# Reordering kv and num on TensorE and moving a copy of v to ScalarE in a linear-attention and MLP kernel

## The chip, the cores and the metric

The kernel runs on one core of a Trainium2 chip. The metric is the device time of one execution in microseconds (us); a version's time is the median of its runs. All runs here are fast, at a granted clock of 0.997 to 1.0. A ratio of two kernels is the mean time of one kernel's fast runs over that of the other's of the same rounds, so it is not quite the ratio of the medians that are quoted beside it. A position in a profile is in us from the start of its span.

Engine names: PE is TensorE (matmul), PEld its weight loads, DVE VectorE, ACT ScalarE, POOL GpSimd, SP the queue that issues most stores and copies. L366 is line 366 of the kernel's file; after the change lines below 190 lie up to 5 further down (L199 is then L202, L366 is L371, L387 is L392), and in e5 4 more. An instruction is "due" at the time at which it would start if nothing but the matmuls ahead of it on TensorE held it up.

## The reference, cut to what matters

```python
# q, k, v: (8 batches, 8 heads, 576 positions, 64)
q_p, k_p = phi(q), phi(k)                      # phi(x) = where(x > 0, x, exp(x) - 1) + 1
kv  = einsum('bhsd,bhse->bhde', k_p, v)
z   = sum(k_p, axis=2)
num = einsum('bhsd,bhde->bhse', q_p, kv)
den = einsum('bhsd,bhd->bhs', q_p, z)[..., None] + 1e-06
x   = (num / den) transposed to (4608, 512)
h   = x @ w_in                                 # layer 1, 2048 wide
out = (h - tanh(h)) @ w_out                    # layer 2
```

## The kernel before

The 4608 rows go through the two layers in 9 chunks of 512. A chunk has a layer 1 of 16 tiles of four matmuls and a layer 2 of 16 steps of four matmuls. The attention of the next batches is hung between them: `s1[i]` holds what is issued behind tile `i` of layer 1, `s2[i]` what is issued behind step `i` of layer 2. The program order is the order on each engine.

```python
def a_qT_pe(b, i, banks, on=None):          # transposes of phi(q), 2 x (matmuls, then a copy by ACT or DVE)
    ...
def a_kv(b, banks):                         # 36 matmuls (64 rows) of kp and v, then kz = kv * mask on DVE
    ...
def a_vp(b, i):                             # v repacked for the later batches
    nc.vector.tensor_copy(vp[:, i, :, 0:128]..., v_b[b % 2][:, 0:2, i])

def a_kv_cols(b, banks):                    # kv from vp, later batches
    ps = [banks()[:, 0:272]... for hg in range(2)]
    for i in range(2):
        for j in range(J):
            for hg in range(2):
                nc.tensor.matmul(ps[hg][:, i, :], kp[...], vp[...], ...)
    for hg in range(2):
        nc.vector.tensor_mul(kz_t[b][:, hg, :, 0:136], ps[hg], mask[...])

def a_den(b, banks):                        # 16 small matmuls with kz, then + 1e-6 and reciprocal on DVE
    ...
def a_spread(b):                            # the reciprocal goes to memory (ds) and comes back on 128 partitions (rdb)
    for t in range(4):
        nc.sync.dma_start(out=ds[:, t, :], in_=rden_t[b][32 * t:32 * t + H, :])
    for hh in range(2):
        nc.sync.dma_start(out=rdb[64 * hh:64 * hh + 64]..., in_=ds[...]...partition_broadcast(64))

def a_num(b, p):                            # num from kz into one of two PSUM banks; DVE scales it by rdb into xT
    ...

# chunk 0 (batch 1)
s2[7].append(lambda: (a_qT_pe(1, 0, side), a_qT_pe(1, 1, side), a_kv(1, side)))
s2[8].append(lambda: b0_scale_rest(side))
s2[9].append(lambda: a_den(1, side))
s2[10].append(lambda: (num1(), a_split(1)))   # split: four DVE steps from the reciprocal to w
s2[11].append(lambda: spread1(0))             # batch 1 is spread by matmuls of w, not through memory
s2[12].append(lambda: q2(0))                  # phi of q of batch 2
...
# chunk 1 (batch 2)
s1[1].append(lambda: a_kphi(2, 1))
s1[3]: a_vp(2, 0), a_vp(2, 1)
s1[7].append(lambda: a_kv_cols(n1, attn))
s1[10].append(lambda: (a_den(n1, attn), a_spread(n1)))
s2[11 + p].append(lambda p=p: a_num(n1, p))   # p = 0 .. 4

# layer 1, behind the four matmuls of tile fi
elif fi % 2:
    n = dense.order[(dense.n - 1) % 6]        # six PSUM banks, three pairs of tiles
    l1act2(fi - 1, ps_all[:, n - 1:n + 1, :], gT)   # tanh on ACT, subtraction on DVE
for f in s1[fi]:
    f()
```

## Time and profile before

| | before |
|---|---|
| median, range of the first 3 runs | 295.44, 295.11 to 295.50 us |
| PE, DVE, ACT busy | 97%, 60%, 48% of the span |
| matmul of 512 columns, start to start | 0.216 us |
| gaps in the PE stream where the change works | 0.72, 0.86 and 0.53 us |

The three gaps are shown and worked out in the prediction below. One more piece of the same kernel's timeline turns out to matter (start, duration, engine, line, operation; in brackets the idle time ahead and what ended it):

```profile
65.45 1.29 SPq L305 DMA_DIRECT2D ds<-rden  x4
70.65 1.12 SPq L308 DMA_DIRECT2D rdb<-ds  x2
...
79.10 1.89 DVE L328 TENSOR_TENSOR xT<-ps_all,rdb 128x512 bf16<-128x512 f32 x3 [2.26 <-DMA rdb<-ds]
...
79.85 0.38 PE L317 MATMUL ps_all<-qT,kz 128*128 128x512 bf16 x1
```

The reciprocal of batch 2 leaves for memory at 65.45, comes back by 79.1, and only then can VectorE scale the first num. The third num needs the PSUM bank of the first. It was due at 79.81 (78.95, the start of the matmuls ahead of it, + 4 x 0.216) and starts at 79.85: before the change, this broadcast is only just on time.

### The profile page before, as it was taken

What the parts mean: (1) busy time and instruction counts of PE and PEld (TensorE: products, weight loads), DVE (VectorE), ACT (ScalarE), POOL (GpSimd) and SP (SyncE); (2) the same over time, 40 slices, a digit from 0 to 9 for tenths busy, and PEclk for the clock granted to TensorE, in tenths of its full rate; (3) what the DMA queues carried; (4) which work ended last, traced back from release to release, by engine and by line L of the source; (5) the groups of instructions that cost most, each with busy time, mean ns of one, the idle gap of its engine ahead of it and who ended that gap; (6) DMA issues with size and microseconds to landing.
All of it is one profiled execution on the core that took longest, in us unless ns stands there. A gap on an engine that the chain in (4) does not pass through costs nothing.

```text
span 293.2 us, 4504 instructions
## 1 busy us (share of the span) xinstructions
PE 285.2 (97%) x1801; PEld 134.3 (46%) x1801; DVE 174.6 (60%) x265; ACT 139.6 (48%) x168; POOL 33.3 (11%) x55
## 2 busy tenths in 40 slices
PE   8899999999999999999999999999999999999994
PEld 2544453454444444444444445444444444444443
DVE  4759857887567764786478646865581456106600
ACT  4938536947344643455246524661552155126411
POOL 8673030030030003000300020000000000000000
PEclk9999999999999999999999999999999999999999
DMA  6999999998999758955895669667117310131032
GB/s 101 194 204 212 208 207 216 200 145 153 234 163 185 160 118 139 218 117 129 136 223 127 139 134 183 134 154 143 38 24 178 73 36 0 38 84 24 0 74 72
DMA packets 39077, 38.94 MB, mean 133 GB/s; under 512 B 16336, under 2 KB 33808, under 8 KB 38288
## 3 DMA queue, kind: packets, MB, share of 16 engines
q0 software_dynamic: 17552, 18.35, 38.6%
q1 hardware_dynamic: 21344, 20.17, 30.3%
q8 instruction: 14, 0.23, 0.3%
q10 hardware_dynamic: 160, 0.13, 0.1%
q14 instruction: 7, 0.06, 0.1%
HBM read 43.91 MB, written 9.55 MB: 182 GB/s over the span
## 4 chain that ended last, share of the span: by engine, by line
PE 79%; DMA 11%; issue 7%; POOL 2%; DVE 0%; ACT 0%; POOLq 0%
PE ps_all L387 37%; PE ps_all L366 36%; DMA qraw<-in_q_dram 6%; DMA w_in_sb<-in_moe_w_in_dram 3%; PE ps_all L199 2%; DMA kraw<-in_k_dram 2%; PE ps_all L317 2%; PE ps_all L604 1%; PE ps_all L276 1%; POOL qraw L90 0%; ACT e L134 0%; POOL kraw L93 0%; DVE qp L136 0%; POOL v L93 0%; POOL w_out_sb L115 0%
## 5 line engine op out<-in xcount | busy, mean ns | idle before, releaser
L366 PE MATMUL ps_all<-xT,w_in_sb 128*128 128x512 bf16 x576 | 128.0, 379 | 0.3 <-DVE xT L244 0.3
L387 PE MATMUL ps_all<-w_out_sb,gT 128*128 128x512 bf16 x560 | 127.8, 379 | 0.0
L373 DVE TENSOR_TENSOR gT<-ps_all,th 128x1024 bf16<-128x1024 f32 x64 | 77.9, 1218 | 59.8 <-ACT th L372 59.8
L372 ACT ACTIVATE th<-ps_all 128x1024 f32<-128x1024 f32 x64 | 65.5, 1024 | 57.0 <-PE ps_all L366 47.1
L366 PEld LDWEIGHTS <-w_in_sb 128*128 128x128 bf16 x576 | 55.3, 98 | 66.6 <-issue 0.6
L387 PEld LDWEIGHTS <-gT 128*128 128x128 bf16 x560 | 54.1, 98 | 64.3 <-issue 0.3
L396 ACT COPY osb<-ps_all 128x512 f32<-128x512 f32 (+1 forms) x36 | 20.9, 583 | 73.4 <-PE ps_all L387 54.2
L328 DVE TENSOR_TENSOR xT<-ps_all,rdb 128x512 bf16<-128x512 f32 x24 | 16.3, 689 | 13.4 <-PE ps_all L317 11.2
L134 ACT ACTIVATE e<-qraw 128x1152 bf16<-128x1152 bf16 x16 | 18.5, 1162 | 6.9 <-DMA qraw<-in_q_dram 6.9
L134 ACT ACTIVATE e<-kraw 128x1152 bf16<-128x1152 bf16 x15 | 17.5, 1166 | 0.2 <-DMA kraw<-in_k_dram 0.2
L136 DVE TENSOR_TENSOR qp<-e,r 128x1152 bf16<-128x1152 bf16 x16 | 12.0, 757 | 7.8 <-ACT e L134 7.2
L136 DVE TENSOR_TENSOR kp<-e,r 128x1152 bf16<-128x1152 bf16 x15 | 11.4, 759 | 8.3 <-ACT e L134 7.5
L383 POOL COPY g<-qT 1x1 bf16<-1x1 bf16 x5 | 1.2, 240 | 120.6 <-DMA qT<-qp 120.6
L378 DVE TENSOR_TENSOR gT<-ps_all,th 128x512 bf16<-128x512 f32 x16 | 10.3, 685 | 2.4 <-ACT th L377 1.7
L377 ACT ACTIVATE th<-ps_all 128x512 f32<-128x512 f32 x16 | 9.2, 598 | 4.3 <-PE ps_all L366 3.1
L317 PE MATMUL ps_all<-qT,kz 128*128 128x512 bf16 x28 | 10.1, 379 | 0.0
L444 PE MATMUL ps_all<-zero 128*128 128x512 bf16 x29 | 8.8, 463 | 1.2 <-DVE zero L405 1.2
L135 DVE TENSOR_SCALAR r<-qraw 128x1152 bf16<-128x1152 bf16 x16 | 7.3, 453 | 2.2 <-DMA qraw<-in_q_dram 2.2
L199 PE MATMUL ps_all<-vp,kp 64*128 64x136 bf16 x216 | 7.4, 220 | 0.4 <-POOL g L383 0.4
L199 PEld LDWEIGHTS <-kp 64*128 64x128 bf16 x216 | 6.4, 94 | 3.0 <-issue 2.1
L285 DVE RECIPROCAL rden<-den 128x144 f32<-128x144 f32 x7 | 7.4, 1053 | 0.2
L394 DVE COPY osb<-ps_all 128x128 f32<-128x128 f32 x1 | 0.3, 292 | 11.6 <-PE ps_all L604 11.6
(82 smaller groups left out, 121.7 us busy)
## 6 DMA issues: line engine op xcount, KB each, us to landing
out_dram<-osb SPq DMA_DIRECT2D x70, 128.0 KB
rdb<-ds SPq DMA_DIRECT2D x12, 576.0 KB
kraw<-in_k_dram POOLq DMA_DIRECT2D x7, 576.0 KB, 7.1
qraw<-in_q_dram POOLq DMA_DIRECT2D x7, 576.0 KB, 9.0
v<-in_v_dram POOLq DMA_DIRECT2D x7, 576.0 KB, 12.2
w_out_sb<-in_moe_w_out_dram POOLq DMA_DIRECT2D x4, 512.0 KB, 16.4
w_in_sb<-in_moe_w_in_dram POOLq DMA_DIRECT2D x6, 256.0 KB, 8.6
qraw<-in_q_dram POOLq DMA_DIRECT2D x2, 288.0 KB, 4.6
```

The lines of the kernel that those rows point to most:

```text
L134: return (lambda: nc.scalar.activation(e, x, AF.Exp), lambda: nc.vector.tensor_scalar(r, x, 0.0, 1.0, ALU.max, ALU.add), lambda: nc.vector ...
L136: lambda: nc.vector.tensor_tensor(y, e, r, ALU.min))
L199: nc.tensor.matmul(ps[hg][:, i, :], kp[r, i, j].rearrange("p h d -> p (h d)"), vp[r, i, j, :], start=(j == 0), stop=(j == J - 1))
L317: nc.tensor.matmul(ps, kz[:, p // 2, p % 2, 0:128], qT[:, p % 2, 0:8, p // 2, :], start=True, stop=True)
L328: nc.vector.tensor_mul(xT[:, p, S * b:S * b + 512].rearrange("p (j t c) -> p j t c", j=8, t=4), ps.rearrange("p j (t c) -> p j t c", t=4), ...
L366: nc.tensor.matmul(h, w_in_sb[:, 2 * (p % 2) + p // 2, fi * 128:(fi + 1) * 128], xT[:, p, c * 512:(c + 1) * 512], start=(n == 0), stop=(n ...
L372: nc.scalar.activation(th, h, AF.Tanh)
L373: nc.vector.tensor_sub(gT[:, fi:fi + 2, :], h, th)
L377: nc.scalar.activation(th, h, AF.Tanh)
L378: nc.vector.tensor_sub(gT[:, fi, :], h, th)
L387: nc.tensor.matmul(o, gT[:, fi, i * 128:(i + 1) * 128], w_out_sb[:, fi, :], start=(fi == 0), stop=(fi == NF - 1))
L396: nc.scalar.copy(osb[:, f0:f1], o[:, f0:f1])
```

## The change

Its intent: fill the wait for phi(q) in chunk 0 with kv, which needs no q; let num run beside den, so that the wait for the num copies closes; in chunk 1, take the copies of v off VectorE, and put kv later and in two halves, so that it does not wait for them.

```diff
+    def a_vp_act(b, i):
+        nc.scalar.copy(vp[:, i, :, 0:128].rearrange("p j (h d) -> p h j d", h=2), v_b[b % 2][:, 0:2, i])
-    def a_kv_cols(b, banks):
+    def a_kv_cols(b, banks, i_s=(0, 1), ps=None):
-        ps = [banks()[:, 0:272].rearrange("p (i e) -> p i e", i=2) for hg in range(2)]
-        for i in range(2):
+        ps = ps or [banks()[:, 0:272].rearrange("p (i e) -> p i e", i=2) for hg in range(2)]
+        for i in i_s:
 (cut: the matmuls)
+        if i_s == (0,):
+            return ps
 (cut: kz)
-            s2[7].append(lambda: (a_qT_pe(1, 0, side), a_qT_pe(1, 1, side), a_kv(1, side)))
+            s2[7].append(lambda: (a_qT_pe(1, 0, side), a_kv(1, side), a_qT_pe(1, 1, side)))
-            s2[9].append(lambda: a_den(1, side))
-            s2[10].append(lambda: (num1(), a_split(1)))
+            s2[9].append(lambda: (a_den(1, side), num1(), a_split(1)))
-            s2[12].append(lambda: q2(0))
-            s2[13].append(lambda: (spread1(1), q2(1)))
-            s2[14].append(lambda: q2(2))
-            s2[15].append(lambda: a_kphi(2, 0))
+            s2[13].append(lambda: (spread1(1), q2(0)))
+            s2[14].append(lambda: q2(1))
+            s2[15].append(lambda: (q2(2), a_kphi(2, 0)))
-            s1[7 if c == 1 else 5].append(lambda: a_kv_cols(n1, attn))
-            s1[10 if c == 1 else 8].append(lambda: (a_den(n1, attn), a_spread(n1)))
+            if c == 1:
+                s1[8].append(lambda: sub.update(kv=a_kv_cols(n1, attn, (0,))))
+                s1[9].append(lambda: a_kv_cols(n1, attn, (1,), sub["kv"]))
+            else:
+                s1[5].append(lambda: a_kv_cols(n1, attn))
+            s1[11 if c == 1 else 8].append(lambda: (a_den(n1, attn), a_spread(n1)))
-            s1[1].append(lambda: a_kphi(2, 1))
-            for i in range(2):
-                s1[3].append(lambda i=i: a_vp(2, i))
+            k21 = phi_pieces(2, k_t, kp_t, "kp", 1)
+            s1[1].append(k21[0])
+            s1[3].append(lambda: (k21[1](), k21[2](), a_vp_act(2, 0)))
+            s1[5].append(lambda: a_vp_act(2, 1))
```

## The prediction

> **What bounds the kernel now.** I read the page first: engine busy times, then the chain that ended last, then TensorE's waits, then the timeline of the two stretches that the change touches, and last the DMA issues with their times to landing.
>
> ```profile
> PE 285.2 (97%) x1801; PEld 134.3 (46%) x1801; DVE 174.6 (60%) x265; ACT 139.6 (48%) x168; POOL 33.3 (11%) x55
> ```
>
> TensorE is busy 97% of 293.2 us, with modelled ends. The chain of waits, from 59 us on, holds almost nothing but matmuls, 64 of a layer in 13.81 us, so 0.216 us each back to back. No matmul is removed by the change. It can only close gaps in TensorE's stream, and can only open others. TensorE's waits name the gaps:
>
> ```profile
> PE ps_all L164 <- DVE qp L136: 0.8, 2, 0.6
> PE ps_all L354 <- ACT ns L344: 0.7, 1, 0.7
> PE ps_all L199 <- POOL g L383: 0.4, 1, 0.4
> ```
>
> All three are in the stretch that the change rearranges. The timeline (start, duration, instruction) shows them in place:
>
> ```profile
> 37.94 0.68 PE L164 MATMUL ps_all<-ident,qp 128*128 128x128 bf16 x9
> 39.17 0.68 PE L164 MATMUL ps_all<-ident,qp 128*128 128x128 bf16 x9 [0.56 <-DVE qp L136]
> 39.78 1.66 PE L177 MATMUL ps_all<-v,kp 64*128 64x192 bf16 x36
> 41.37 1.04 PE L387 MATMUL ps_all<-w_out_sb,gT 128*128 128x512 bf16 x4
> ...
> 46.17 0.37 DVE L298 SCALAR_TENSOR_TENSOR w<-t,part,u 128x144 bf16<-128x144 bf16 x1
> 47.26 0.31 PE L354 MATMUL ps_all<-w,sel 32*128 32x144 bf16 x8 [0.69 <-ACT ns L344]
> ...
> 51.30 7.07 PE L366 MATMUL ps_all<-xT,w_in_sb 128*128 128x512 bf16 x32
> ...
> 58.23 0.82 DVE L189 COPY vp<-v 128x1152 bf16<-128x1152 bf16 x2
> 58.74 1.24 PE L199 MATMUL ps_all<-vp,kp 64*128 64x136 bf16 x36 [0.37 <-POOL g L383]
> ```
>
> Gap one: the first nine transposes take 9 x 0.057, to 38.45; the next come at 39.17: 0.72. Gap two: the matmuls before the spread (L354) end at 46.40, it starts at 47.26: 0.86; the reciprocal's split is done at 46.54, the last num copy at 47.20. Gap three: layer 1 runs 32 x 0.216 from 51.30, to 58.21, and kv starts at 58.74: 0.53. The label says GpSimd, but its gate feeds only loads; what kv reads is vp, whose first half VectorE ends at 58.64. Together 2.1 us, 0.7% of the time: the most that can be won.
>
> **What the Trainium skill says.** "Trace Analysis", section Per-instruction lifecycle, says that the profiled window of a GpSimd-issued DMA ends when descriptors are generated, not when data has moved. So arrival must be read from the times to landing. These two loads are issued at 22.28 and 23.01:
>
> ```profile
> v<-in_v_dram POOLq DMA_DIRECT2D x1, 576.0 KB, 16.5
> w_out_sb<-in_moe_w_out_dram POOLq DMA_DIRECT2D x1, 512.0 KB, 18.3
> ```
>
> v of batch 1 lands at 38.8, and the third quarter of w_out, which the layer-2 matmuls after kv read, at 41.3. "ScalarE: Activation LUTs", section What ACT_TABLE_LOAD costs, gives 186 ns + 0.833 ns per element, with 93 ns overlap of neighbours: 1146 ns for 1152 elements. The trace agrees: its exp of 1152 takes 1.16 to 1.20, start to start 1.06. Nothing shows this copy on ScalarE before, so I take the exp's figure for it. The same page's Rules for kernel authors has VectorE up to about 3x faster for bf16; here the vp copy on VectorE is 0.45, a factor of 2.6. "TensorEngine Tiling (Array Packing)", section Key Properties, says that changing the tiling mode drains TensorE. The trace fits: in an undisturbed chunk kv takes 1.17 to the next dense matmul, where 36 x 0.0287 (136 columns, two row tiles at once, at 0.42 ns per column, as 512 columns in 0.216) is 1.03; so leaving it costs about 0.15.
>
> ```profile
> 87.46 1.17 PE ps_all L199 x36
> 88.63 2.70 PE ps_all L366 x12
> 91.33 0.36 PE ps_all L276 x16
> ```
>
> **The change, part by part.** The instruction order per engine confirms the same matmuls, reordered; VectorE loses two vp copies, ScalarE gains two.
>
> *Chunk 0, kv between the transposes.* kv needs v, and that lands at 38.8, so it starts at about 38.85, not 38.46. With its 1.59 (39.78 to 41.37 now) it ends at 40.44; the second transposes take 0.51, to about 41.0. But the next layer-2 matmuls need w_out, landing at 41.3. They start at about 41.36, as now at 41.37. So gap one only moves: 0.3 before kv, 0.3 before those matmuls. Gain: 0.
>
> *num beside den.* den stays at 43.3, so its VectorE work to w still ends at 46.54. num comes 0.86 earlier (four matmuls), at 43.7, and its copies end at 46.3, no longer last. The two layer-2 groups now follow num and end at 43.3 + 0.36 + 0.1 + 0.97 + 1.73, about 46.5. The spread starts behind w at 46.68, not 47.26. Gain: 0.58. Layer 1 of chunk 1 starts at 50.72. Moving the query work of batch 2 one step later brings ScalarE into this order: eviction, exp, eviction, exp, eviction, exp of k; at its spacings now (0.47, 1.06) the last eviction starts at 51.93 and the exp at 52.40.
>
> *Chunk 1, vp on ScalarE.* The first tanh runs at 53.46, the second exp of k at 54.36, the second tanh at 55.42 to 56.44, the first copy at 56.32, tanh, the second copy at 58.28, ended by 59.45. The kernel gives layer 1 six PSUM banks, three pairs of tiles: the seventh tile needs the first subtraction, ended at 54.54 + 1.22 = 55.76; it is due at 50.72 + 24 x 0.216 = 55.90, so it just passes. The ninth needs the second subtraction, ended at 57.72; due at 57.63: wait of about 0.15. Gap three (0.53) is gone, since kv comes behind the ninth tile at 58.64.
>
> *kv in two halves.* A second tiling change, 0.15. First half 58.64 to 59.30, tile ten to 60.17, second half to 60.83, tiles eleven and twelve to 62.56, den due at 62.67. Here I see a new wait. den needs kz, the masked product on VectorE. In the new order it stands behind the subtraction of tiles nine and ten. That one follows their tanh (60.37 to 61.39) and the earlier subtraction (60.42 to 61.55): it runs from 61.55, kz from 62.68 to 63.46. den's last twelve matmuls wait for this and end at 63.78 instead of 63.03: 0.75. Now kz starts at 61.23 and den (62.60) does not wait.
>
> Sum: -0.58 - 0.53 + 0.15 + 0.15 + 0.75 = -0.06, with about 0.1 to 0.2 of error in the terms. Layer 2 of chunk 1 starts at about 67.4, as now at 67.46. From there all is the same. With the time before at 295.44, I predict 295.2, leaning a little to the gain because two of my losses (0.15 and 0.75) rest on a chain of starts and the gain rests on one.
>
> **The rivals.** *All gaps close* (the intent): -2.0, 293.4. Against it stand the two landings and w's own end. *The landings don't bind*, if kv may start at 38.46 and w_out is in time: den comes about 0.7 earlier, the spread near 46.0, 294.5. For it: landing times may vary by tenths, and now nothing waits there. Against: the load queue is full throughout (its share is 1.23 of 16 engines between 20 and 40 us), and the change touches no earlier load. *kz is not late*, if VectorE catches up: 294.5. Against: the order puts tanh, subtraction, kz one behind the other, 3.3 us after tile ten, and den only 2.5 us after it. *ScalarE becomes the bound of the start of chunk 1*: the seventh tile has 0.14 of slack; a copy slower than 1.15, or a late eviction, makes each following tile wait: 296 or a little over. For it: ScalarE has 2.1 us more work within the first ten tiles.
>
> **Range and chances.** The rivals lie between 293.4 and 296; the likeliest two misses (each 0.7 to 0.9) go opposite ways. So 294.2 to 296.0 in 8 of 10. A change of 2% would be 5.9 us, almost three times all gaps there are: faster 0.01, within 2% 0.98, slower 0.01.
>
> **What the profile after should show.** The wait at L164 for qp gone; kv in chunk 0 waiting for the load of v until 38.8; the first layer-2 matmuls behind the transposes still at 41.3 to 41.4; the spread 0.5 to 0.7 earlier and released by w, not by the num copies; no wait for vp; two ScalarE copies of about 1.15 each; den of chunk 1 waiting about 0.7 for kz; layer 2 of chunk 1 within 0.4 of 67.46. I am wrong if that stage starts before 66.9 (a landing or kz was no limit) or after 68 (ScalarE holds up PSUM).

## The result, and the profile after

| | before | after |
|---|---|---|
| median of 4 runs of the same rounds | 295.27 us | 295.60 us |
| range | 294.72 to 295.50 | 295.51 to 295.71 |
| ratio after to before | | 1.0014 (95%: 0.9997 to 1.0031) |
| the same kernel again in later rounds (e11) | | 1.0027 (1.0015 to 1.0040) |

The time is inside the predicted range and class, but a few tenths of a us above the kernel before, where I had leaned to a few tenths below. In the first rounds that loss is not clear of noise (the interval holds 1); in those of e11 it is. The waits of TensorE in the changed kernel (us in total, times, longest) no longer have the three of before:

```profile
PE ps_all L322 <- DVE xT L333: 0.5, 1, 0.5
...
PE ps_all L281 <- DVE kz L207: 0.3, 1, 0.3
PE ps_all L392 <- DMA w_out_sb<-in_moe_w_out_dram: 0.2, 1, 0.2
```

In their place stand a wait of den (L281) for kz, one of layer 2 for the load of w_out, and one of num (L322) for the scaling of an earlier num. The timeline of the changed kernel, with the same places as in the prediction and those of the new waits:

```profile
38.29 0.67 PE L164 MATMUL ps_all<-ident,qp 128*128 128x128 bf16 x9
...
39.02 1.43 PEld L177 LDWEIGHTS <-kp 64*128 64x128 bf16 x36 [0.25 <-DMA v<-in_v_dram]
...
40.62 0.68 PE L164 MATMUL ps_all<-ident,qp 128*128 128x128 bf16 x9
...
41.53 1.02 PE L392 MATMUL ps_all<-w_out_sb,gT 128*128 128x512 bf16 x3 [0.24 <-DMA w_out_sb<-in_moe_w_out_dram]
...
46.75 0.12 PEld L359 LDWEIGHTS <-sel 32*128 32x128 bf16 x8 [0.53 <-DVE w L303]
...
58.35 1.19 ACT L192 COPY vp<-v 128x1152 bf16<-128x1152 bf16 x1
...
58.80 0.71 PE L202 MATMUL ps_all<-vp,kp 64*128 64x136 bf16 x18
...
62.77 0.78 DVE L207 TENSOR_TENSOR kz<-ps_all,mask 128x272 bf16<-128x272 f32 x2
...
63.26 0.72 PE L281 MATMUL ps_all<-qT,kz 128*32 128x144 bf16 x16 [0.31 <-DVE kz L207]
```

The chunk-0 half does as foreseen: kv waits for v, layer 2 behind the transposes for w_out, and the spread (L359) is released by w. In chunk 1 den comes due at 62.88 (eight matmuls from 61.05, and 0.1) and ends at 63.91 instead of 63.24: 0.67 for kz. Later in the same timeline:

```profile
66.60 1.29 SPq L310 DMA_DIRECT2D ds<-rden  x4
...
71.42 1.12 SPq L313 DMA_DIRECT2D rdb<-ds  x2
...
79.77 1.89 DVE L333 TENSOR_TENSOR xT<-ps_all,rdb 128x512 bf16<-128x512 f32 x3 [2.85 <-DMA rdb<-ds]
80.51 0.38 PE L322 MATMUL ps_all<-qT,kz 128*128 128x512 bf16 x1 [0.46 <-DVE xT L333]
```

The reciprocal leaves 1.15 us later than before and its broadcast is back 0.67 later (0.95 and 0.47 on the common scale of the next paragraph), and the third num, due at 79.89 (79.03 + 4 x 0.216), starts at 80.51: 0.62 where it was 0.04.

Two profiles of one kernel differ by 0.2 to 0.3 us in when the first loads land (the exp named below starts at 36.12 in the changed kernel and at 35.94 in e11, at 35.67 in e6 and at 35.94 in e13). To compare stages I take the start of each from the start of the exp of q of batch 1 (35.92 before, 36.12 after), which begins when that load lands, ahead of all that the change touches. In every run below the spread starts within 0.03 us of one of three values on this scale, so tenths can be read from it.

| start, us after that exp | spread | layer 1 of chunk 1 | layer 2 of chunk 1 | layer 1 of chunk 2 |
|---|---|---|---|---|
| before | 11.34 | 15.38 | 31.38 | 46.20 |
| after | 10.64 | 14.68 | 31.25 | 46.66 |
| difference | -0.70 | -0.70 | -0.13 | +0.46 |

So chunk 0 gains 0.70, layer 1 of chunk 1 gives back 0.57, and its layer 2 loses 0.59 more. From there on the two kernels run alike: from the start of that layer to the end of the span it is 211.1 us before and 211.0 after.

### The profile page after: what moved, and what is told of

The parts are those of the page before. It is cut to its first block, busy times and chain, and to the rows that moved or that the text cites. A ratio compares the mean times of both kernels' runs of the same rounds, so it can differ in the third digit from the quotient of the medians.

```text
span 293.8 us, 4469 instructions
## 1 busy us (share of the span) xinstructions
PE 284.6 (97%) x1772; PEld 134.3 (46%) x1801; DVE 174.2 (59%) x263; ACT 141.6 (48%) x170; POOL 33.4 (11%) x55
## 4 chain that ended last, share of the span: by engine, by line
PE 78%; DMA 15%; POOL 2%; issue 2%; DVE 1%; SPq 0%; ACT 0%; DVEq 0%; POOLq 0%
PE ps_all L371 37%; PE ps_all L392 35%; DMA w_out_sb<-in_moe_w_out_dram 6%; DMA w_in_sb<-in_moe_w_in_dram 3%; DMA rdb<-ds 3%; PE ps_all L202 2%; DMA kraw<-in_k_dram 2%; PE ps_all L322 2%; DMA ds<-rden 1%; PE ps_all L612 1%; PE ps_all L281 1%; POOL v L424 1%; POOL qraw L90 0%; DVE rden L290 0%; PE ps_all L325 0%
## 5 line engine op out<-in xcount | busy, mean ns | idle before, releaser
L392 PE MATMUL ps_all<-w_out_sb,gT 128*128 128x512 bf16 x547 | 126.1, 379 | 0.9 <-DMA w_out_sb<-in_moe_w_out_dram 0.2
L322 PE MATMUL ps_all<-qT,kz 128*128 128x512 bf16 x28 | 10.1, 379 | 0.5 <-DVE xT L333 0.5
```

What stands on the lines that cost most here:

```text
L322: nc.tensor.matmul(ps, kz[:, p // 2, p % 2, 0:128], qT[:, p % 2, 0:8, p // 2, :], start=True, stop=True)
L392: nc.tensor.matmul(o, gT[:, fi, i * 128:(i + 1) * 128], w_out_sb[:, fi, :], start=(fi == 0), stop=(fi == NF - 1))
```

## The experiments

My theory after the result: the gaps that the change closes each had another limit right behind them, and the loss is the broadcast of the reciprocal of batch 2, made late by den (one step later, 0.67 behind kz, and behind a subtraction on VectorE). Rivals: the wait for kz is itself the loss; the copies on ScalarE cost too much; the two halves are independent. Twelve runs were made, of ten new kernels and two repetitions (e11, e13). "Ratio" is always to the kernel before in the same rounds.

| run | ratio (95%) | spread | layer 1 of chunk 1 | layer 2 of chunk 1 | layer 1 of chunk 2 |
|---|---|---|---|---|---|
| e1 chunk-0 half | 0.9994 (0.9982 to 1.0006) | 10.67 | 14.71 | 31.08 | 46.12 |
| e2 chunk-1 half | 1.0023 (1.0010 to 1.0036) | 11.33 | 15.37 | 31.75 | 46.94 |
| e3 kz first | 1.0025 (1.0013 to 1.0037) | 10.66 | 14.70 | 30.61 | 47.08 |
| e4 num late | 1.0001 (0.9989 to 1.0013) | 10.67 | 14.71 | 31.29 | 46.13 |
| e5 no landings | 1.0001 (0.9986 to 1.0016) | 10.25 | 14.29 | 30.87 | 45.93 |
| e9 kz and den first | 0.9990 (0.9978 to 1.0003) | 10.67 | 14.71 | 30.62 | 45.95 |
| e6 both, num late | 0.9980 (0.9967 to 0.9992) | 10.65 | 14.69 | 30.60 | 45.39 |
| e7 vp on VectorE | 1.0038 (1.0025 to 1.0052) | 10.66 | 14.70 | 31.79 | 47.55 |
| e10 no loads of batch 3 | 0.9992 (0.9979 to 1.0006) | 10.66 | 14.71 | 31.28 | 46.08 |
| e11 the change again | 1.0027 (1.0015 to 1.0040) | 10.65 | 14.70 | 31.28 | 46.65 |
| e12 mended chunk 1 alone | 0.9994 (0.9981 to 1.0006) | 11.34 | 15.38 | 31.15 | 45.95 |
| e13 e6 again | 0.9976 (0.9963 to 0.9990) | 10.65 | 14.69 | 30.60 | 45.39 |

### e1 and e2: each half alone

e1 is the kernel before with the five changed lines of chunk 0 (`s2[7]` to `s2[15]` in the diff above); e2 is the changed kernel with these lines as before.

> The chunk-0 half of the change alone (kv between the transposes, num beside den, query work of batch 2 one step later); chunk 1 as in the kernel before. My theory: layer 1 of chunk 1 starts 0.5 us earlier (50.8 instead of 51.30), but vp of chunk 1 is made on VectorE behind a chain that starts with ScalarE's evictions and exps, and that chain is no earlier, so kv of chunk 1 still starts at about 58.6 and its gap grows from 0.53 to about 1.0: the gain is given back within 8 us. Layer 2 of chunk 1 starts within 0.2 of the kernel before; time 0.0 to 0.2 us below it. Rival (the gain is kept, and only the chunk-1 half costs): 0.5 us below the kernel before.

> The chunk-1 half alone (vp copied by ScalarE, kv in two halves behind tiles nine and ten, den one step later); layer 2 of chunk 0 as in the kernel before. My theory: no wait for vp, but den waits about 0.7 us for kz and the broadcast of the reciprocal lands later by some 0.7 us, so that the third num matmul of batch 2 waits too: 0.5 to 0.9 us above the kernel before. Rival (the two halves of the change are independent, and each saves its own gap): 0.3 to 0.5 us below it.

e1's layer 1 of chunk 1 starts at 50.94, so kv, 32 matmuls later, is due at 57.85. Its timeline:

```profile
58.75 1.24 PE L199 MATMUL ps_all<-vp,kp 64*128 64x136 bf16 x36 [0.75 <-DVE vp L189]
```

The gap ahead of kv has grown from 0.53 to 0.90: more than half of the 0.67 gained in chunk 0 is given back there (my theory had said nearly all; layer 2 of chunk 1 starts 0.30 earlier, not within 0.2), and 0.22 more at num (15.04 from layer 2 to the next layer 1, against 14.82). What is left at chunk 2, 0.08, is not clear of noise in the times. So the gap that the chunk-1 half is meant to close gets wider by the chunk-0 half. By itself (e2) the chunk-1 half costs 0.37 up to layer 2 and 0.37 in it, within the expected 0.5 to 0.9: it holds the loss, and does not save its own gap as the rival had it. How far the halves act on one another is a smaller matter: e1 and e2 add up to +0.66 at chunk 2 (-0.08 and +0.74), and both together give +0.46; the times alone do not tell the two apart.

### e3: kz ahead of the subtraction

```diff
+                pair = ps_all[:, n - 1:n + 1, :]
+                if c == 1 and fi in (9,):
+                    for f in s1[fi]:
+                        f()
+                    s1[fi] = []
-                l1act2(fi - 1, ps_all[:, n - 1:n + 1, :], gT)
+                l1act2(fi - 1, pair, gT)
```

> The changed kernel with kz placed on VectorE ahead of the subtraction of tiles nine and ten. My theory: den's wait for kz (about 0.65 us with its two parts) goes and layer 2 of chunk 1 starts at about 66.7 instead of 67.4; but the reciprocal still stands behind the subtraction of tiles eleven and twelve, its broadcast lands when it does now (79.6), and the wait of the third num matmul grows from 0.5 to about 1.1 us: time within 0.15 us of the changed kernel. Rival (the wait for kz is a cost by itself): 0.65 us below the changed kernel.

In e3's list of waits that for kz is gone, and the one of num is three times as long:

```profile
PE ps_all L322 <- DVE xT L333: 1.5, 1, 1.5
```

Layer 2 of chunk 1 starts 0.64 earlier than in the changed kernel (30.61 against 31.25), and nothing of it is left at chunk 2. The ratio, 1.0025, lies between the two of the changed kernel (1.0014 and 1.0027). The wait for kz, which I had taken for the main cost, is real, but as long as the broadcast is late it costs nothing: whoever is early in layer 1 waits for the broadcast in layer 2. The broadcast came back 0.4 later here than in the changed kernel with the reciprocal at the same place (VectorE takes it up at 44.06 on the common scale, against 43.65). The scatter lies in the second stage, from the issue of `rdb<-ds` on (8.72 us here, 8.35 there; the first stage takes 4.84 and 4.82); it is not explained.

### e4: num one step later

```diff
-                s2[(11 if c == 1 else 9) + p].append(lambda p=p: a_num(n1, p))
+                s2[min(12 + p, 15) if c == 1 else 9 + p].append(lambda p=p: a_num(n1, p))
```

> The changed kernel with the num matmuls of batch 2 one step (four matmuls, 0.86 us) later in layer 2 of chunk 1, the last two in one step. My theory, that the late landing of the broadcast reciprocal costs 0.5 us: no wait of the third num matmul (perhaps 0.1 at the start of chunk 2 for the last scaling), 0.4 to 0.5 us below the changed kernel, a little below the kernel before. Rival (that wait is not on the path, the loss is elsewhere): same time as the changed kernel.

e4's timeline at the third num:

```profile
79.60 1.89 DVE L333 TENSOR_TENSOR xT<-ps_all,rdb 128x512 bf16<-128x512 f32 x3 [3.15 <-PE ps_all L322]
...
80.35 0.38 PE L322 MATMUL ps_all<-qT,kz 128*128 128x512 bf16 x1
```

No wait of num; layer 1 of chunk 2 starts 0.53 earlier than in the changed kernel, and the ratio falls to 1.0001. So the late broadcast is on the path, and it is the loss. I had hoped for a little below the kernel before; the ratio does not show it. Part of the reason is that the later num has a price of its own: in the four runs with it (e4, e6, e12, e13) the first 24 matmuls of chunk 2 take 5.52 us instead of 5.34, and from the start of chunk 2 to the end of the span it is 211.17 to 211.24 us, where all other runs have 210.98 to 211.09. So about 0.2 has to be taken off what these four runs gain in the last column of the table.

### e9 and e6: kz and den first, without and with the later num

Both as e3 with `fi in (9, 11)`, so that den's addition and reciprocal also go ahead of a subtraction; e6 has e4's line too.

> The changed kernel with kz ahead of the subtraction of tiles nine and ten, and den's addition and reciprocal ahead of that of tiles eleven and twelve. The reciprocal is then done at about 64.3 instead of 66.6. Theory A (the broadcast goes through the memory queue behind the loads of batch 3, which fill it until about 70): it lands 0.5 us earlier at most, num still waits about 0.9, time 0.3 to 0.5 us below the changed kernel. Theory B (the broadcast just takes as long as it takes): it lands 2 us earlier, no wait of num, time 1.2 us below the changed kernel.

> The same order on VectorE, and num of batch 2 one step later as in the run before that had it: no wait for kz and none, or under 0.3 us, for the broadcast. 1.0 to 1.3 us below the changed kernel and 0.6 to 1.0 us below the kernel before (about 294.2): the version that beats both if the two waits are all that the change lost. If some third thing holds layer 2 of chunk 1, it stays at 294.9.

e9's timeline:

```profile
64.76 1.29 SPq L310 DMA_DIRECT2D ds<-rden  x4
...
70.59 1.12 SPq L313 DMA_DIRECT2D rdb<-ds  x2
...
78.90 1.89 DVE L333 TENSOR_TENSOR xT<-ps_all,rdb 128x512 bf16<-128x512 f32 x3 [2.77 <-DMA rdb<-ds]
79.65 0.38 PE L322 MATMUL ps_all<-qT,kz 128*128 128x512 bf16 x1 [0.38 <-DVE xT L333]
```

The reciprocal leaves 1.84 us earlier than in the changed kernel, the broadcast is back 0.87 earlier (1.69 and 0.72 on the common scale; its first stage now takes 5.83 us to the issue of the second, not 4.82): closer to theory A than to B, though its gain was under-called (0.7 at chunk 2 where I said 0.3 to 0.5). With num later as well (e6) no wait of num is left, layer 1 of chunk 2 starts 1.27 before that of the changed kernel and 0.81 before that of the kernel before (1.05 and 0.65 at the end of the span). Against e4, which differs only in the order on VectorE, it starts 0.74 earlier: with num out of the way, kz and den first do pay. e6 and its repetition e13 are the only runs whose interval lies below the kernel before: 0.9980 and 0.9976, medians 294.35 and 294.14 us.

### e10: the broadcast without the loads of batch 3

```diff
-            s1[0].append(lambda: (gate(qT_t[n1]), load_k(n2), load_q(n2), load_v(n2)))
+            if c == 1:
+                k_t[n2], q_t[n2] = k_t[n1], q_t[n1]
+            else:
+                s1[0].append(lambda: (gate(qT_t[n1]), load_k(n2), load_q(n2), load_v(n2)))
```

> The changed kernel without the loads of k, q and v of batch 3 in chunk 1, so with a wrong result on purpose (it goes on with old data). If the broadcast of the reciprocal of batch 2 is late because it waits behind these loads, its first stage lands about 2 us after issue instead of 4 to 5, and the whole lands 2 us or more earlier than 79.6 with the same reciprocal (66.6): no wait of num, 0.5 us below the changed kernel. If the broadcast takes its 13 us by itself, it lands at 79.6 as before and the wait of 0.5 us stays.

e10's timeline of the first stage:

```profile
66.23 1.29 SPq L310 DMA_DIRECT2D ds<-rden  x4
68.56 1.12 SPq L313 DMA_DIRECT2D rdb<-ds  x2
```

and the row of 66 to 68 us in the table by stretches (length, then busy time and count of PE, PEld, DVE, ACT and POOL, granted clock, share of the 16 DMA engines, GB/s), in the changed kernel and in e10:

```profile
66.00:68.00 2.00, 2.00 (x11) 0.88 (x9) 1.67 (x2) 1.30 (x2) 0.00 (x0) 1.00 1.20 205
```

```profile
66.00:68.00 2.00, 2.00 (x11) 0.91 (x10) 1.42 (x2) 1.30 (x2) 0.00 (x0) 1.00 0.04 8
```

and e10's first scaling:

```profile
77.78 0.69 DVE L333 TENSOR_TENSOR xT<-ps_all,rdb 128x512 bf16<-128x512 f32 x1 [1.23 <-PE ps_all L322]
```

With the DMA engines all but idle (their share, which the view can give above 1, is 0.04 instead of 1.20) the first stage takes 2.33 us from its first issue to the issue of the second, not 4.82; the broadcast is back before 77.8, when VectorE takes it up without waiting, and the wait of num is gone (46.08 at chunk 2, 0.58 less than in the changed kernel). The Trainium skill, page "Trainium Kernel Development and Optimization", section Key Constraints, says that transfers issued from SP, ACT and POOL run on the same 16 engines and interleave; this pair of runs agrees and gives the price here, 2.5 us for 18 KB. So the broadcast is late for two reasons: den, and a queue of loads that fills the engines until about 70 (their share is 0.14 between 70 and 72 us in the changed kernel). Only the first is the change's doing: the same loads are there in the kernel before (share 1.20 from 66 to 68, 1.05 from 68 to 70).

### e5: kv and layer 2 of chunk 0 without their loads

The edit, shortened:

```diff
+                rhs = vt[r, :, i, j, :]; for b == 1: kp flattened, [r, 64 * j:64 * j + 192]   # no v
-                                 vt[r, :, i, j, :], start=(j == 0), stop=(j == J - 1))
+                                 rhs, start=(j == 0), stop=(j == J - 1))
-            l2mm(gT, os_[i], i, 4 * g, 4 * g + 4)
+            l2mm(gT, os_[i], i, 4 * g, 4 * g + 4, 4 if c == 0 and g == 2 else 0)   # second quarter of w_out
```

> The changed kernel with two loads taken out of the path, with a wrong result on purpose: kv of batch 1 reads kp in place of v, and the third quarter of layer 2 of chunk 0 reads the second quarter of w_out. Same matmuls, same shapes. My theory (the landings of v and w_out hold gap one open): no wait for v or w_out, kv starts right behind the first transposes, the layer-2 matmuls that now start 3.25 us after the first transposes start 2.6 us after them, and the spread is some 0.6 us earlier in relation to the first transposes. At the end little of it is left, because the broadcast of the reciprocal of batch 2 lands nearly as now: its wait grows from 0.5 to about 1 us, time 0 to 0.3 us below the changed kernel. Rival (the matmuls there are held by something else): no shift of the spread.

The result is wrong on purpose (relative error 1.6 million). e5's timeline:

```profile
37.91 0.67 PE L164 MATMUL ps_all<-ident,qp 128*128 128x128 bf16 x9
38.51 1.66 PE L181 MATMUL ps_all<-kp 64*128 64x192 bf16 x36
40.10 0.68 PE L164 MATMUL ps_all<-ident,qp 128*128 128x128 bf16 x9
40.83 0.81 PE L396 MATMUL ps_all<-w_out_sb,gT 128*128 128x512 bf16 x3
41.48 0.28 PE L329 MATMUL ps_all<-qT,kz 128*128 128x64 bf16 x4
```

The waits for v and w_out are gone, and the layer-2 matmuls start 2.7 us behind the first transposes (four matmuls ahead of 41.48, one record being missing), not 3.24. The spread comes 0.39 earlier on the common scale (0.55 measured from the first transposes, where I had said 0.6). So the two landings do hold gap one open. What I expected of the end was wrong: num's wait shrank to 0.27 (it starts at 79.24, due at 78.97) instead of growing, and chunk 2 begins 0.73 earlier than in the changed kernel. Layer 1 of chunk 1 moved up by 0.39, and with it the reciprocal (30.09 on the common scale, not 30.48) and what the loads of batch 3 wait for, the transposed q and phi of k of batch 2: they are issued at 58.27, 22.69 on the common scale, not 59.19 (23.07). The broadcast is back at 78.49, 0.74 earlier on the common scale. Of this 0.39 is the reciprocal's own; the other 0.35 would fit loads that are through earlier, but is no more than the scatter seen in e3, so it is not shown.

### e7: the copies of v back on VectorE

```diff
-            s1[3].append(lambda: (k21[1](), k21[2](), a_vp_act(2, 0)))
-            s1[5].append(lambda: a_vp_act(2, 1))
+            s1[3].append(lambda: (k21[1](), k21[2](), a_vp(2, 0)))
+            s1[5].append(lambda: a_vp(2, 1))
```

> The changed kernel with the two vp copies on VectorE at the same places (kv in two halves as in the change). My theory: ScalarE is not the bound in that stage, and the copy on VectorE stands behind r and the minimum of k: kv's first half starts 0.5 us later than in the changed kernel, kz and den follow, 0.4 to 0.7 us above the changed kernel. Rival (1.2 us per copy on ScalarE delays the tanh and costs more than 0.45 on VectorE): 0.3 us or more below the changed kernel.

kv waits for vp again:

```profile
PE ps_all L202 <- DVE vp L189: 0.5, 1, 0.5
```

With that, layer 2 of chunk 1 starts 0.54 later than in the changed kernel and chunk 2 0.89 later. A copy of 1.19 us on ScalarE was the better choice than one of 0.45 on VectorE, because the latter stands behind phi of k. ScalarE was not the bound. My estimate of 0.4 to 0.7 was a little low.

### e11, e12, e13: the change again, and the mended version with and without the chunk-0 half

> The changed kernel itself, for comparison on this chip: ratio to the kernel before 1.001 to 1.002, and in its profile a wait of 0.3 for kz and of about 0.5 for the broadcast.

> The mended chunk 1 (kz and den first, num late) with layer 2 of chunk 0 as in the kernel before. If the chunk-0 half saves its 0.5 us wherever nothing later binds, this is 0.4 to 0.6 us slower than the run that has both, so 0.0 to 0.3 us below the kernel before. If the chunk-0 half is worth nothing, it equals the run that has both.

> The run with both halves and the mended order again, beside the one without the chunk-0 half on the same chip: ratio to the kernel before 0.997 to 0.999.

e11 repeats the changed kernel: 1.0027, a little above what I expected, and a profile whose stages agree with the first to 0.03. e12 has the diff lines of chunk 0 as before and e6's other lines; it starts chunk 2 0.56 later than e13, and is at 294.68 us against 294.14. So the chunk-0 half is worth its half us once nothing behind it takes it back. The mended chunk 1 by itself is not shown to gain: it starts chunk 2 0.25 before the kernel before, but the later num takes some of it back (0.13 is left at the end of the span), and its interval holds 1.

## Why the prediction was right or wrong

**Right, and shown.** (The page that the prediction calls "Trace Analysis" has the title "Perfetto Trace Analysis".) The two landings in gap one: both waits appear (0.25 for v, 0.24 for w_out), and e5 removes them. The spread released by w: predicted gain 0.58, measured 0.70 (the matmul follows w by 0.06 instead of my 0.14, and den is 0.05 earlier). Gap three gone; e7 shows that moving kv is not enough for this: with the copies on VectorE at the same places kv waits 0.5 again, so it takes the move and ScalarE's copies together. kz late behind the subtraction: predicted 0.75, measured 0.67. The wait ahead of tile nine and the costs of leaving the tiling mode: kv was foreseen at 58.64 and starts at 58.80, of which 0.08 is layer 1's later start (50.80, not 50.72). ScalarE's copies: 1.18 and 1.19 for the 1.15 I took, and 1.04 to 1.05 to the start of the next instruction. The sum up to layer 2 of chunk 1: predicted -0.06, measured -0.13.

**Wrong.** The step that failed is "From there all is the same." I moved den and lengthened its path on VectorE, and did not follow its product on. The reciprocal of batch 2 goes through memory to num, and the profile of before had the line for it: VectorE idle for 2.26 us until rdb came. A term of +0.59 is missing from my sum. It turned a gain of 0.1 into a loss of 0.46 in the profile, 0.14% and 0.27% in the two sets of runs (0.4 and 0.8 us; only the second is clear of noise). That the range held it is due to its width, which was set for other misses: in this point it was luck. The sign that I had named, layer 2 of chunk 1 within 0.4 of 67.46, came true (67.37); what failed lies behind it.

**Also wrong** was what I made of kz. I named 294.5 for the case that kz is not late. e3 is that case, and it stands at 1.0025: removing a wait ahead of another wait gains nothing by itself. And my last sentence of the sum, that I leaned to the gain because one chain is surer than two, was a guess without ground.

**Left open.** Why the broadcast lands up to 0.4 us apart in runs with the same reciprocal (e3 and the changed kernel), and what its second stage, some 8 us for 1.15 MB, is made of, was not tested. (The packets in the kept traces narrow it down: the stage's 128 packets of 9216 B begin 1.3 us after its issue in both runs, run for 6.0 us in the changed kernel and 6.5 in e3, and VectorE starts 0.9 to 1.1 us after the last of them.) Nor was what makes den late taken apart further: den at its old place, or kv in one piece behind the ninth tile, was not run. Nor was another order of the early loads that would bring v and w_out in sooner.

## What to carry to other kernels

In this kernel, busy 97% on one engine, each of the three gaps met another limit within 0.8 us once its first was out of the way (v and w_out after phi of q, w after the num copies, a PSUM bank and kz after vp). So list for each gap the second and third limit and when each would release. Follow the product of every operation that is moved to its last reader, through memory too: here the loser was 17 us behind den (63.26 to 80.51), held by a broadcast that had only just been on time. And a wait is worth removing only if the next one on the path has slack: e3 took away 0.67 us and gained nothing, until e6 moved the next one too.

## What the Trainium skill lacked or had wrong

- "Trainium Kernel Development and Optimization", section Key Constraints: it says that transfers of several queues interleave on the same engines, and gives no figure for what a small one pays behind large ones. Here 18 KB to memory took 4.82 us from issue to the next stage's issue behind loads that filled the engines (share 1.20), and 2.33 without them.
- "TensorEngine Tiling (Array Packing)", section Key Properties: a change of tiling mode drains the engine; no cost is given. Here it is some 0.15 us for leaving the 64-row mode, an estimate (1.17 us from the start of kv to the next dense matmul, less the 1.03 reckoned for its 36 matmuls).
- "ScalarE: Activation LUTs", section Rules for kernel authors: its first row sends relu, max, min, add and mul to VectorE because that is faster per element; a copy is not named. For the single copy this held (0.45 us against 1.19), but the row does not ask what stands ahead on the engine: with the copies on VectorE e7 starts chunk 2 0.89 us later than the changed kernel.
